# Attention and gated MLP on one Trainium2 core: scores in pairs of tiles, every weight tile turned by DMA, and one division for two heads

## The chip, the cores and the metric

The kernel runs on one core of one Trainium2 chip. The metric is the device time of one execution in microseconds, lower is better. The kernel before takes 2773.86 us (median of three runs, 2771.83 to 2776.18).

## The reference

One transformer block with adaptive layer norm, batch 1, 2048 rows of width 576, all in float32:

```
mod = silu(c) @ w_mod ; sa, ca, ga, sb, cb, gb = six rows of 576
h = layernorm(x) * (1 + ca) + sa
q = h @ wq                                   # 32 heads of 128
k, v = last 512 rows of the caches           # 16 heads, each serves two q heads
p = softmax(q k^T / sqrt(128)) ; o = p v
x = x + ga * (o @ wo)
h = layernorm(x) * (1 + cb) + sb
out = x + gb * ((silu(h @ w1) * (h @ w3)) @ w2)   # hidden width 4608
```

## The kernel before

**Numbers in two halves.** Each float32 operand is split into a high and a low float16 half, and a product is made of three float16 matmuls: high-high, high-low, low-high.

**Attention is cut into 128 slots.** A slot is one query head with one block of 512 rows (`slots`, line 449). Two slots in a row (`j` 0 and 1) are the two heads that share a key head. Each slot has four steps `t`, one for each tile of 128 query rows. The work of several slots is interleaved by the loop at lines 1558 to 1604. Every engine, and SyncE's queue, runs its instructions strictly in the order in which this loop issues them, so the order written there is the schedule. In slot `i` the loop issues:

- `scores(i, t)` in each step (line 475): three matmuls of 512 columns into one bank `pss`; VectorE takes the negated maximum of each row (487) and scales it (488).
- `weights(i, t)` (491): ScalarE takes the exponential out of the bank and sums it (500). For tiles 0 to 2 `half_high` (529) makes the float16 high half on ScalarE and `half_low` (534) the low half on GpSimd; `turn_away` (539) has a DMA transpose, issued by SyncE, turn both halves into the tile `ptw`. Tile 3 is turned by four TensorE transposes (`turn`, 517); ScalarE and VectorE take it out of the bank as high and low halves (525, 549).
- `query(i + 1, part)` (455): 14 matmuls that make the next slot's queries, in three parts (`QP`, 441), then their halves on ScalarE (467) and VectorE (473).
- `values(i - 1)` at the end of the slot (554): 12 matmuls of 512 columns. The first of them already reads all four turned tiles.
- `sums(i - 1, step)` (503): the reciprocal of the row sums, its way through memory (510) and back, spread over all partitions (513).
- `normalize(i - 2)` (567) multiplies the output by that on VectorE; `split_on(i - 2)` (577) in step 3 makes its halves, high on ScalarE (581), low on GpSimd (582).
- `attend_out`, one call in each step (584): six matmuls of 288 columns with `wo`, into the one double bank `E`, and every second step VectorE adds the result to the residual (590).

**The MLP's weights are prepared meanwhile.** Slots 13 to 123 also carry 168 pieces of work that split the weights of the MLP (lines 725 to 736 and 1304 to 1332 give each its due step). A piece of a set of `w1`/`w3` is a ScalarE cast (768) and two GpSimd subtractions (769, 770). `run(i, t)` issues them at the end of a step. After the slots the MLP runs alone.

**Banks.** The eight PSUM banks are `E` (two), `A` (two, for queries and outputs), `S` (two, for scores) and `T` (two, for transposes). `T` also serves the turning of normalized rows (`turn_rows`, 236).

## Time and profile before

| | |
|---|---|
| runs | 2771.83, 2773.86, 2776.18 us |
| the profiled execution | 2773.59 us, span 2771.7 us |
| attention, slots 0 to 127 | 33 to about 1610 us |
| busy TensorE, VectorE, ScalarE, GpSimd | 97%, 72%, 58%, 68% of the span |
| DMA transposes | 384, median 3.9 us from issue to landing |

The profile is one execution, seen by the hardware profiler. Its page gives busy times by engine, the span in 40 slices, and the costliest groups of instructions by line. Other views list groups by form, waits, stretches of time, or instructions in order of time; there a row gives start, duration, engine, line, operation, and out and in operands, and rows of several like instructions are merged (x12). TensorE's matmuls overlap, so the time from start to start is what one costs, not its duration. `PEld` is TensorE's weight load, `POOL` is GpSimd, `ACT` is ScalarE, `DVE` is VectorE and `SPq` is the queue of SyncE.

### The profile page before, as it was taken

What the parts mean: (1) busy time and instruction counts of PE and PEld (TensorE: products, weight loads), DVE (VectorE), ACT (ScalarE), POOL (GpSimd) and SP (SyncE); (2) the same over time, 40 slices, a digit from 0 to 9 for tenths busy, and PEclk for the clock granted to TensorE, in tenths of its full rate; (3) what the DMA queues carried; (4) which work ended last, traced back from release to release, by engine and by line L of the source; (5) the groups of instructions that cost most, each with busy time, mean ns of one, the idle gap of its engine ahead of it and who ended that gap; (6) DMA issues with size and microseconds to landing.
All of it is one profiled execution on the core that took longest, in us unless ns stands there. A gap on an engine that the chain in (4) does not pass through costs nothing.

```text
span 2771.7 us, 44752 instructions
## 1 busy us (share of the span) xinstructions
PE 2692.8 (97%) x15406; PEld 1515.9 (55%) x15406; DVE 1999.8 (72%) x3555; ACT 1617.5 (58%) x3013; POOL 1881.9 (68%) x1748
## 2 busy tenths in 40 slices
PE   6899999999999999999999999999999999999998
PEld 3455555555555555555555555555555555555554
DVE  7877787877788787877876667777776666666666
ACT  5777778777777778787677634544443333333332
POOL 5578788888788877777669537688873465333435
PEclk8999999999999999999999999999999999999999
DMA  5778888788787788979889935656643434333332
GB/s 184 174 174 195 196 177 192 169 184 192 160 185 167 191 186 201 206 182 213 184 190 223 239 112 171 200 170 199 213 135 108 160 121 128 104 103 111 104 110 78
DMA packets 593460, 463.84 MB, mean 167 GB/s; under 512 B 442704, under 2 KB 472528, under 8 KB 592208
## 3 DMA queue, kind: packets, MB, share of 16 engines
q1 hardware_dynamic: 592944, 460.69, 64.9%
q8 instruction: 121, 1.98, 0.3%
q14 instruction: 107, 0.88, 0.1%
q10 hardware_dynamic: 288, 0.30, 0.0%
HBM read 264.19 MB, written 95.99 MB: 130 GB/s over the span
## 4 chain that ended last, share of the span: by engine, by line
PE 52%; DVE 2%; issue 1%; ACT 1%; POOL 1%; DMA 0%; SPq 0%; DVEq 0%; ACTq 0%; POOLq 0%
PE py L847 15%; PE px L847 11%; PE pe L932 7%; PE pf L932 7%; PE pe L433 3%; PE po L562 3%; PE pss L483 3%; PE pq L410 2%; PE pt L523 0%; PE pq L414 0%; DVE table L487 0%; DVE acc L590 0%; DVE on L571 0%; DMA r<-row 0%; ACT p L500 0%
## 5 line engine op out<-in xcount | busy, mean ns | idle before, releaser
L537 POOL TENSOR_TENSOR hp<-p,hp 128x512 f16<-128x512 f32 x384 | 450.2, 1175 | 271.0 <-ACT hp L532 147.9
L500 ACT ACTIVATE p<-pss,table,factors 128x512 f32<-128x512 f32 x512 | 396.9, 775 | 360.9 <-DVE table L488 186.6
L847 PEld LDWEIGHTS <-wset 128*128 128x128 f16 x3528 | 344.6, 98 | 337.9 <-issue 5.3
L487 DVE TENSOR_REDUCE table<-pss 128x1 f32<-128x512 f32 x512 | 350.3, 684 | 209.9 <-PE pss L483 205.9
L847 PE MATMUL py<-hset,wset 128*128 128x512 f16 x2016 | 483.6, 380 | 0.0
L433 PE MATMUL pe<-o 128*128 128x288 f16 x3072 | 459.6, 286 | 15.8 <-DVE acc L590 15.3
L483 PE MATMUL pss<-k,qT 128*128 128x512 f16 x1536 | 420.1, 381 | 13.7 <-ACT p L500 10.3
L433 PEld LDWEIGHTS <-o 128*128 128x128 f16 x3072 | 300.7, 98 | 189.6 <-issue 22.4
L562 PE MATMUL po<-ptw,v 128*128 128x512 f16 x1536 | 359.3, 382 | 10.4 <-DVE ptw L552 5.5
L847 PE MATMUL px<-hset,wset 128*128 128x512 f16 x1512 | 361.6, 379 | 1.6 <-ACT p L500 1.6
L410 PE MATMUL pq<-hT,wq 128*128 128x512 f16 x1092 | 283.2, 382 | 1.0 <-POOL hT L254 0.7
L94 POOL TENSOR_TENSOR akv<-u,akv 128x512 f16<-128x512 f32 x141 | 165.0, 1180 | 174.3 <-ACT akv L93 166.5
L532 ACT CAST hp<-p 128x512 f16<-128x512 f32 x384 | 237.3, 618 | 13.2 <-POOL hT L256 0.6
L562 PEld LDWEIGHTS <-v 128*128 128x128 f16 x1536 | 148.2, 98 | 175.4 <-issue 19.4
L932 PEld LDWEIGHTS <-akv 128*128 128x128 f16 x1728 | 169.6, 98 | 93.8 <-issue 4.8
L483 PEld LDWEIGHTS <-qT 128*128 128x128 f16 x1536 | 147.9, 98 | 129.0 <-issue 15.6
L590 DVE SCALAR_TENSOR_TENSOR acc<-pe,factors,acc 128x576 f32<-128x576 f32 x256 | 207.7, 811 | 10.4 <-PE pe L433 10.4
L582 POOL TENSOR_TENSOR o<-on,o 128x512 f16<-128x512 f32 x128 | 150.4, 1175 | 55.6 <-ACT o L581 52.7
L410 PEld LDWEIGHTS <-wq 128*128 128x128 f16 x1092 | 107.5, 98 | 129.7 <-issue 4.6
L926 DVE SCALAR_TENSOR_TENSOR acc<-pf,table,acc 128x576 f32<-128x576 f32 x140 | 113.4, 810 | 80.3 <-PE pf L932 80.3
L1027 ACT COPY u<-py 128x512 f32<-128x512 f32 x72 | 42.2, 586 | 202.1 <-PE py L847 200.2
L1020 ACT ACTIVATE s<-s,table 128x512 f32<-128x512 f32 x72 | 52.0, 722 | 173.9 <-DVE s L1019 173.9
(244 smaller groups left out, 4791.2 us busy)
## 6 DMA issues: line engine op xcount, KB each, us to landing
wset<-wd SPq DMA_DIRECT2D x213, 320.0 KB, 3.2
r<-row SPq DMA_DIRECT2D x128, 256.0 KB, 3.9
oset<-od SPq DMA_DIRECT2D x106, 288.0 KB, 3.2
wraw<-in_w SPq DMA_DIRECT2D x36, 768.0 KB, 5.7
wd<-wmade SPq DMA_DIRECT2D x75, 320.0 KB, 3.3
wset<-wd SPq DMA_DIRECT2D x71, 160.0 KB, 2.3
w2raw<-in_w SPq DMA_DIRECT2D x19, 576.0 KB, 5.3
wd<-ring SPq DMA_DIRECT2D x33, 320.0 KB, 2.8
```

Of the source, the lines that this page charges most:

```text
L94: eng.tensor_sub(halves[:, 1], src, halves[:, 0])
L410: nc.tensor.matmul(ps, w[:, k // 2, m, :], hT[:, DC + m if k == 1 else m, :], start=s == 0, stop=False)
L433: nc.tensor.matmul(E[:, h, :HALF], o[:, x, rows], w[:, y, h * HALF : (h + 1) * HALF], start=first and n == 0, stop=last and n == 2,)
L483: nc.tensor.matmul(pss, q[:, x, rows], k[:, y, :], start=n == 0, stop=n == 2)
L487: nc.vector.tensor_reduce(nm[:, 0:1], pss, axis=AX.X, op=ALU.max, negate=True)
L500: nc.scalar.activation(p, pss, AF.Exp, bias=nm[:, 1:2], scale=factor, accum_out=st["l"][:, t : t + 1])
L532: nc.scalar.copy(hp[:, 0, :], state[i]["p", t])
L537: nc.gpsimd.tensor_sub(hp[:, 1, :], state[i].pop(("p", t)), hp[:, 0, :])
L562: nc.tensor.matmul(po, v[:, x, c, :], pt[:, y, c, :], start=c == 0 and n == 0, stop=c == KC - 1 and n == 2)
L590: nc.vector.scalar_tensor_tensor(a, E[:, :, :HALF], factors[:, uses[u][0], 2:3], a, op0=ALU.mult, op1=ALU.add)
L847: nc.tensor.matmul(ps, w[:, a, :], h[:, b, :], start=start and n == 0, stop=stop and n == 6, skip_group_check=True)
L932: nc.tensor.matmul(ps[:, h, :HALF], a[:, rows], w[:, b, :], start=m == 0, stop=m == 2)
```

## The change

Four edits belong together:

- **Pairs.** `scores` is issued in steps 0 and 2 only, each time for two tiles, into a pair of banks; one VectorE reduction gives the maxima of both tiles and one instruction scales them. `weights` and `half_high` for both follow in steps 1 and 3. The pairs come from the pool `T`, now two pairs of banks; `S` is gone until the attention has ended.
- **All tiles by DMA.** `turn`, `turn_high` and `turn_low` go. All four tiles pass `half_high`, `half_low` and `turn_away`. The low halves of tiles 0 and 1 are issued at the start of step 2, those of tiles 2 and 3 at the start of the next slot.
- **Low half on VectorE.** The low half of a slot's tile 0 is VectorE's, from slot 3 on.
- **Ratio of sums.** The first head of a pair isn't normalized: ScalarE (`take_first`, step 0) and VectorE make its halves straight from the bank. The second is multiplied by the ratio of the two row sums, and the first head's reciprocal is applied when the result is added to the residual. Reciprocal, row and its return happen once for two slots.

The three parts of the query become 4, 6 and 4 matmul groups instead of 5, 5 and 4.

```diff
-    QP = (range(0, 5), range(5, 10), range(10, 14))
+    QP = (range(0, 4), range(4, 10), range(10, 14))
...
-        pss = bank("S", "pss")
-        for n, (x, y) in enumerate(((0, 0), (0, 1), (1, 0))):
-            nc.tensor.matmul(pss, q[:, x, rows], k[:, y, :], start=n == 0, stop=n == 2)
...
+        pss = pair_bank("pss")
+        for half in range(2):
+            rows = slice((t + half) * P, (t + half + 1) * P)
+            for n, (x, y) in enumerate(((0, 0), (0, 1), (1, 0))):
+                nc.tensor.matmul(pss[:, half, :], q[:, x, rows], k[:, y, :], start=n == 0, stop=n == 2)
...
-        nc.vector.tensor_reduce(nm[:, 0:1], pss, axis=AX.X, op=ALU.max, negate=True)
-        nc.vector.tensor_scalar(nm[:, 1:2], nm[:, 0:1], factor, P_LOG, op0=ALU.mult, op1=ALU.add)
+        nc.vector.tensor_reduce(nm[:, 0:2], pss, axis=AX.X, op=ALU.max, negate=True)
+        nc.vector.tensor_scalar(nm[:, 2:4], nm[:, 0:2], factor, P_LOG, op0=ALU.mult, op1=ALU.add)
...
+        if j == 0:
+            return
         if step == 0:
-            nc.vector.reciprocal(st["l"][:, ST:], st["l"][:, :ST])
+            nc.vector.reciprocal(up, both)
+            nc.vector.scalar_tensor_tensor(ratio, first, O_DOWN, up[:, ST:], op0=ALU.mult, op1=ALU.mult)
...
-        nc.gpsimd.tensor_sub(hp[:, 1, :], state[i].pop(("p", t)), hp[:, 0, :])
+        eng = nc.vector if t == 0 and i > 2 else nc.gpsimd
+        eng.tensor_sub(hp[:, 1, :], state[i].pop(("p", t)), hp[:, 0, :])
...
+    def take_first(i):
+        st = state[i]
+        o = st["o"] = new_o(i)
+        nc.scalar.activation(o[:, 0, :], st["po"], AF.Copy, scale=O_DOWN)
...
     def normalize(i):
         st = state[i]
         po = st.pop("po")
+        if slots[i][1] == 0:
+            o = st["o"]
+            nc.vector.scalar_tensor_tensor(o[:, 1, :], po, O_DOWN, o[:, 0, :], op0=ALU.mult, op1=ALU.subtract)
+            return
...
     for i in range(n + 2):
         run(i, -1)
         for t in range(ST):
+            if t == 0 and 1 <= i <= n:
+                half_low(i - 1, 2)
+                half_low(i - 1, 3)
+            if t == 2 and i < n:
+                half_low(i, 0)
+                half_low(i, 1)
             if t > 1 and i < n:
                 turn_away(i, t - 2)
-            if t == 0 and 1 <= i <= n:
-                turn_away(i - 1, 2)
-            slot, tile = (i - 1 if t == 1 else n, ST - 1)
-            if 0 <= slot < n:
-                turn(slot, tile)
-            if i < n:
+            if t < 2 and 1 <= i <= n:
+                turn_away(i - 1, t + 2)
+            if t % 2 == 0 and i < n:
                 scores(i, t)
...
-            if 1 <= i <= n and t == 2:
-                turn_low(i - 1, ST - 1)
...
-            if i < n:
-                weights(i, t)
-            if t < 3 and i < n:
-                half_high(i, t)
-                half_low(i, t)
-            if t == 1 and 1 <= i <= n:
-                turn_high(i - 1, ST - 1)
+            if t % 2 and i < n:
+                for k in (t - 1, t):
+                    weights(i, k)
+                    half_high(i, k)
+            if 2 <= i <= n + 1 and t == 0 and slots[i - 2][1] == 0:
+                take_first(i - 2)
```

More of the change, by code (lines that the diff above doesn't have):

```diff
@@ L578, in split_on @@
         st = state[i]
+        if slots[i][1] == 0:
+            return
         on = st.pop("on")
-        o = st["o"] = pool.tile([P, 2, SB], F16, tag=("ah", "al")[i % 2], name="o", bufs=3)
+        nc.vector.tensor_scalar(
+            st["l"][:, 5 * ST :], st["l"][:, 2 * ST : 3 * ST], factors[:, uses[slots[i][0]][0], 2:3], 1.0 / O_DOWN,
+            op0=ALU.mult, op1=ALU.mult,
+        )
+        o = st["o"] = new_o(i)
         nc.scalar.copy(o[:, 0, :], on)
@@ L1515, in tile_block @@
         norm_rows(0, t)
-    turned = [turn_rows(0, m, "TTAAS"[m]) for m in range(DC + 1)]
+    firsts = [pair_bank(), pair_bank()]
+    junk = firsts[1][:, 1, :]
+    turned = [
+        turn_rows(0, m, "A", None if m in (2, 3) else firsts[m // 4][:, m % 2, :]) for m in range(DC + 1)
+    ]
     for m in range(DC + 1):
@@ L1607, in tile_block @@
     lane[1] = (E, after.tile([P, 2, 512], F32, tag="T2", name="pf"))
+    later.append(after)
     for _ in stream:
```

53 lines of the change are left out of this document (25 added, 28 removed).

## The prediction

> **What bounds the kernel now.** I read the page first, then busy time by stretches, then one slot in order of time, then groups by line.
>
> ```profile
> span 2771.7 us, 44752 instructions
> ...
> PE 2692.8 (97%) x15406; PEld 1515.9 (55%) x15406; DVE 1999.8 (72%) x3555; ACT 1617.5 (58%) x3013; POOL 1881.9 (68%) x1748
> ...
> PE   6899999999999999999999999999999999999998
> ...
> DMA  5778888788787788979889935656643434333332
> ```
> ```profile
> 242.30:1008.80 766.50, 751.38 (x4289) 418.65 (x4288) 600.71 (x1209) 596.13 (x1154) 651.76 (x627) 1.00 0.80 181
> 1008.80:1293.60 284.80, 280.73 (x1605) 156.16 (x1604) 226.17 (x458) 217.64 (x427) 217.99 (x196) 1.00 0.87 199
> ```
>
> TensorE is busy nearly everywhere. The stretch rows give slots 16 to 79 and 80 to 103: length, then busy TensorE, its weight load, VectorE, ScalarE, GpSimd, clock, DMA share. In the first, TensorE is busy for 98%, VectorE and ScalarE for 78%, GpSimd for 85%, and the DMA engines for 0.80. So TensorE's list of matmuls bounds the attention, at the full clock (1.00), with GpSimd and the DMA engines not far behind. The stretch has 64 slots, so one lasts 766.5 / 64 = 11.98 us. The change leaves the MLP as it is, so only the attention counts.
>
> A slot without delay, in order of time (first column: start):
>
> ```profile
> 611.82 0.81 PE L483 MATMUL pss<-k,qT 128*128 128x512 f16 x3
> ...
> 613.54 0.90 PE L433 MATMUL pe<-o 128*128 128x288 f16 x6
> ...
> 614.28 0.60 PE L523 MATMUL pt<-ident,p 128*128 128x128 f32 x4
> ...
> 614.72 0.81 PE L483 MATMUL pss<-k,qT 128*128 128x512 f16 x3
> ...
> 620.83 2.75 PE L562 MATMUL po<-ptw,v 128*128 128x512 f16 x12
> ...
> 623.42 0.81 PE L483 MATMUL pss<-k,qT 128*128 128x512 f16 x3
> ```
>
> From start to start, twelve matmuls of 512 columns take 2.59 us, 0.216 each; six of 288 take 0.74; the four transposes of tile 3 take 0.44. One slot (611.82 to 623.42) lasts 11.60: 38 x 0.216 + 4 x 0.74 + 0.44 = 11.61. The 0.4 us between that and 11.98 are delays and small other matmuls.
>
> **What the change takes from TensorE.** The four transposes of each of 128 slots: 128 x 0.44 = **56 us**, if nothing else becomes late. A slot would be 11.17. Everything else on TensorE stays.
>
> **The other engines, per slot.**
>
> ```profile
> L537 POOL TENSOR_TENSOR hp<-p,hp 128x512 f16<-128x512 f32 x384 | 450.2, 1175 | 271.0 <-ACT hp L532 147.9 <-issue 81.7 <-DVE table L488 14.2
> ...
> L487 DVE TENSOR_REDUCE table<-pss 128x1 f32<-128x512 f32 x512 | 350.3, 684 | 209.9 <-PE pss L483 205.9 <-PE pe L310 3.2
> ...
> L582 POOL TENSOR_TENSOR o<-on,o 128x512 f16<-128x512 f32 x128 | 150.4, 1175 | 55.6 <-ACT o L581 52.7 <-DMA h<-hf 0.9 <-POOL wmade L770 0.7
> ...
> L571 DVE TENSOR_TENSOR on<-po,r 128x512 f32<-128x512 f32 x128 | 139.0, 1086 | 17.0 <-POOL o L582 8.3 <-DMA r<-row 7.0 <-PE po L562 1.8
> ...
> L488 DVE TENSOR_SCALAR table<-table,factors 128x1 f32<-128x1 f32 x512 | 109.6, 214 | 18.2
> ...
> L769 POOL TENSOR_TENSOR wmade<-wraw,wmade 128x512 f16<-128x512 f32 x99 | 107.1, 1081 | 1.4 <-ACT wmade L768 1.0
> ...
> L552 DVE TENSOR_TENSOR ptw<-pt,ptw 128x512 f16<-128x512 f32 x128 | 87.5, 684 | 27.3 <-ACT ptw L527 25.7 <-DMA od<-omade 1.2
> ...
> L581 ACT CAST o<-on 128x512 f16<-128x512 f32 x128 | 78.1, 610 | 7.1 <-DVE on L571 7.1
> ...
> L768 ACT CAST wmade<-wraw 128x768 f16<-128x768 f32 x99 | 74.4, 751 | 0.0
> ...
> L1126 DVE TENSOR_REDUCE peak_cols<-wraw 128x1 bf16<-128x768 f32 x72 | 67.8, 941 | 0.0
> ...
> L770 POOL TENSOR_TENSOR wmade<-wraw,wmade 64x256 f16<-64x256 f32 x99 | 64.0, 647 | 7.8
> ...
> L1162 DVE TENSOR_REDUCE peak_cols<-w2raw 128x1 bf16<-128x1152 f32 x19 | 25.6, 1346 | 0.1
> ```
>
> - VectorE: a maximum over 1024 columns isn't in the trace; between 941 (768 columns) and 1346 (1152) it is 1.21 us. Two of them for four of 684 save 0.31, two scalings of 214 less save 0.43. Tile 3's low half out of a bank (684) becomes tile 0's out of SBUF: 0.74 to 1.08, by rows further down. A first head's low half is like L552 (684) where 1086 stood: 0.20 a slot. Reciprocal, ratio and factor are a few tiny ones per pair. Net -0.6 us: no new bound.
> - ScalarE swaps one copy for another: nothing.
> - GpSimd keeps three low halves of 1175 a slot and loses L582 for every second slot: -0.59 us.
> - SyncE issues one more transpose, and half the rows of sums and returns. Its other transfers are loads due ten steps later and stores; they can wait.
> - The DMA engines carry a fourth transpose. At 0.80 of 11.98 they work 9.6 us a slot for three transposes and all the rest, so one costs at most 3.2; its 256 KB at the stretch's 181 GB/s are 1.4. Half a return of 256 KB goes. I take +1: (9.6 + 1) / 11.9 = 0.89, and 0.96 from slot 80 on. No bound yet, but landings get later.
>
> **What becomes late: the last tile.** The outputs of slot i (the twelve matmuls) need all four tiles. Tile 3 took a short way over TensorE. Now tiles 2 and 3 go through one long chain. Its pieces, from two other places of the same stretch:
>
> ```profile
> 615.56 0.69 DVE L487 TENSOR_REDUCE table<-pss 128x1 f32<-128x512 f32 x1 [1.49 <-PE pss L483]
> ...
> 616.79 1.16 POOL L537 TENSOR_TENSOR hp<-p,hp 128x512 f16<-128x512 f32 x1
> ...
> 616.99 0.77 ACT L500 ACTIVATE p<-pss,table,factors 128x512 f32<-128x512 f32 x1
> ...
> 617.89 0.62 ACT L532 CAST hp<-p 128x512 f16<-128x512 f32 x1
> ...
> 619.42 0.69 DVE L487 TENSOR_REDUCE table<-pss 128x1 f32<-128x512 f32 x1
> ...
> 620.45 0.78 ACT L500 ACTIVATE p<-pss,table,factors 128x512 f32<-128x512 f32 x1 [0.21 <-POOL hp L537]
> ```
> ```profile
> L544 SPq DMA_TRANSPOSE ptw<-hp x384: 1232/1238/4019, 41.5 to 1592.4; - x192
> ...
> DMA to landing us min/median/max: 3.0/3.9/8.2
> ```
>
> 1. Scores of tiles 2 and 3: six matmuls, 1.29, then 0.2 to the maximum (614.72 + 3 x 0.216 to 615.56). 2. The maximum, 1.21. 3. From its end to the exponential 0.34 (620.11 to 620.45), which holds the scaling. 4. Exponential and high half of a tile, 616.99 to 618.51: 1.52, twice 3.04. Together 6.1. VectorE is late by some 0.5: it must first do tile 0's low half, which stands ahead of this maximum in its queue and itself waits for tile 0's high half and for the residual of step 1. So 6.6.
> 5. GpSimd. Its low halves of tiles 2 and 3 are issued at the start of the next slot, behind all that step 3 gave it. In an even slot that is at best nothing: 1.2 after the last high half. In an odd slot `split_on` stands ahead of them: ScalarE makes that copy after tile 3's high half (0.61), GpSimd then needs 3 x 1.175: **4.2** in all. 6. A transpose takes 1.24 to issue and lands after a median of 3.9 us.
>
> Even slots: 6.6 + 1.2 + 3.9 = 11.7. Odd: 6.6 + 4.2 + 3.9 = 14.7. TensorE meanwhile does, from the start of those scores: 1.29, four query matmuls 0.86, two pieces of `wo` 1.48, values 2.59, then the next slot up to its values: 8.57 (11.17 less 2.59). In all **14.8**. So an even slot has 3 us to spare and an odd one nothing.
>
> A piece of weight preparation in step 3 stands in the same place: 0.75 on ScalarE, then 1.08 + 0.65 on GpSimd. An odd slot becomes 14.7 + 1.73 = 16.4, late by 1.6; an even one 6.6 + 0.75 + 1.73 + 2.35 + 3.9 = 15.3, late by 0.5. By the due times some 48 of the slots 13 to 123 have such a piece in step 3. Sum: 24 odd ones x 1.6 = 38, 24 even x 0.5 = 12, and the 40 other odd ones x 0.4 = 16 (half of the transposes land after the median, up to 8.2). **66 us** of new waits at the values.
>
> **Small terms.**
>
> ```profile
> PE pss L483 <- ACT p L500: 10.3, 15, 2.5
> ...
> PE po L562 <- DVE ptw L552: 5.5, 8, 2.9
> ```
>
> These waits (us, times, longest) go: a pair has two steps until its bank is wanted, and L552 is gone. **-16.** But the turned rows of later blocks, 20 banks of four transposes each, now share the two pairs with the scores. Between nothing and one exponential with its cast (1.5 us) each, I take 0.6: **+12**.
>
> Sum: -56 + 66 - 16 + 12 = +6. Against the profiled execution (2773.59, beside a median of 2773.86): **2780 us**. What TensorE is spared comes back as a wait for the last tile.
>
> **Rivals.**
>
> *The chain fits.* If the chain is 3 us shorter than I think (VectorE not late, GpSimd's list of step 3 mostly done before the last high half, landings at 3.0), the waits vanish: 2773.6 - 56 - 16 + 12 = **2714**; up to 2745 with the waits of the odd slots with a piece partly left. For it: in the trace GpSimd is idle for 271 us ahead of L537, so it has room. This is the side faster than before; it decides if the last transpose lands within 14.8 us of its scores.
>
> *The chain is a microsecond longer.* Then plain odd slots cost 1.2 each (40 x 1.2 = 48), odd ones with a piece 2.6 (62), even ones with a piece 1.5, of which the preceding slot's wait gives back a third (24): 134 - 56 - 16 + 12 = +74, and less some 20 of other delays that are hidden behind these waits: about **2828**. For it: VectorE's new subtraction of two SBUF operands beside GpSimd's:
>
> ```profile
> 611.78 0.92 DVE L386 SCALAR_TENSOR_TENSOR k<-kvraw,us,k 128x512 f16<-128x512 f32 x1
> ...
> 612.24 1.48 POOL L537 TENSOR_TENSOR hp<-p,hp 128x512 f16<-128x512 f32 x1
> ...
> 623.90 0.74 DVE L367 SCALAR_TENSOR_TENSOR v<-kvraw,us,v 128x512 f16<-128x512 f32 x1
> ```
>
> Where both overlapped, GpSimd took 1.48 for 1.16 and VectorE 0.92 for the 0.74 of a like one. The Trainium skill, SBUF — State Buffer, section "SBUF: two separate sides", says that a VectorE operation with two SBUF inputs and a GpSimd operation that reads SBUF exclude each other for a whole instruction; the rows agree in kind. By that rule tile 0's low half can wait for a whole 1.16 and the chain grows by it: this rival's time. DMA shares near 0.96 from slot 80 on speak for it too.
>
> *Nothing to gain.* TensorE's spared time is idle anyway, because jitter of the others sets the slots: within 5 us of **2774**. Against it: many slots run at the 11.6 of the matmuls alone.
>
> **How the numbers follow.** Chances: forecast 0.45 (its own range 2755 to 2808, half a microsecond of chain either way), chain fits 0.30, chain longer 0.15, nothing 0.10. About 0.2%, 5.5 us, is what a measurement can tell. The forecast's range lies for 0.12 below that, 0.12 within, 0.21 above; with the rivals: faster 0.12 + 0.30 + 0.03, same 0.12 + 0.04, slower 0.21 + 0.15 + 0.03. The range from 2714 to 2826 leaves out half of the longest-chain case and a little below the shortest.
>
> **What would show it.** Right: slots of 11.2 us where nothing waits, with no L523; TensorE's longest wait is for `ptw<-hp` ahead of the values, about 50 to 90 us in all, mostly in odd slots and where step 3 has a piece of weights; the pair's maximum takes 1.2. Wrong: that wait is under 20 us and the attention ends near 1555 (the chain fits), or transposes land after 5 us and slots reach 12.5 (the chain is longer), or the wait is elsewhere, ahead of the scores.

## The result and the profile after

| | median us | runs | ratio to before (95% interval) |
|---|---|---|---|
| before | 2772.85 | 2771.61 to 2776.18 (4) | |
| after | 2930.76 | 2927.36 to 2935.35 (4) | 1.0569 (1.0547 to 1.0590) |

The change makes the kernel 5.7% slower, 158 us. The forecast was 2780, with a range up to 2826. The profiled execution of the changed kernel took 2934.12 us.

From the page of the changed kernel:

```profile
span 2932.3 us, 42840 instructions
...
PE 2689.8 (92%) x14894; PEld 1465.9 (50%) x14894; DVE 2066.0 (70%) x3104; ACT 1633.6 (56%) x3013; POOL 1832.6 (62%) x1687
...
PE   6898989879898988989989879999999999999998
...
PE 56%; POOL 12%; DVE 8%; DMA 7%; issue 7%; ACT 3%; SPq 1%; POOLq 0%; ACTq 0%; DVEq 0%
...
L562 PE MATMUL po<-ptw,v 128*128 128x512 f16 x1536 | 406.0, 420 | 176.8 <-DMA ptw<-hp 118.9
L497 DVE TENSOR_REDUCE table<-pss 128x2 f32<-128x1024 f32 x256 | 311.8, 1218 | 333.0 <-PE pss L493 332.3
```

512 instructions left TensorE, as forecast, but its digits in slices 3 to 24, all 9 before, are now 7 to 9, and the chain that ended last, 52% TensorE before with nothing else above 2%, now runs through GpSimd (12%), VectorE (8%) and the DMA engines (7%). Before, the row of the values (L562) read:

```profile
L562 PE MATMUL po<-ptw,v 128*128 128x512 f16 x1536 | 359.3, 382 | 10.4 <-DVE ptw L552 5.5
```

The next fences show the attention and the rest of the span as two stretches, before and after (length, then busy TensorE, weight load, VectorE, ScalarE, GpSimd, granted clock, DMA share, GB/s).

```profile
33.00:1613.20 1580.20, 1533.28 (x8711) 855.97 (x8712) 1211.05 (x2450) 1173.08 (x2271) 1220.96 (x1156) 0.99 0.81 187
1613.20:2771.70 1158.50, 1142.16 (x6618) 647.57 (x6615) 763.26 (x1049) 428.69 (x718) 645.73 (x567) 1.00 0.43 138
```
```profile
33.00:1774.60 1741.60, 1532.71 (x8200) 807.18 (x8200) 1278.50 (x2001) 1189.84 (x2271) 1171.82 (x1096) 0.96 0.79 179
1774.60:2932.30 1157.70, 1140.56 (x6617) 646.92 (x6615) 763.33 (x1050) 428.44 (x718) 645.19 (x567) 1.00 0.44 138
```

The MLP is unchanged. The attention is 161 us longer, although 56 us of transposes are gone, so 217 us came in. Two columns of the L562 rows account for nearly all of it: idle time ahead of the values rose from 10.4 to 176.8, and the values' own matmuls from 359.3 to 406.0, together 213 us. The second part goes with the granted clock, which fell from 0.99 to 0.96. In the trace of the kernel after, the twelve matmuls of the values take 2.37 us from the first start to the last in 85 of the slots 8 to 117, at a granted clock of 1.00, and 3.6 to 4.7 us in the other 25, at 0.50 to 0.66. Of these 25, 24 stand behind more than 2.2 us of idle time, and in the 60 slots with less than 1 us of it the clock is always 1.00. So the lower clock follows the long waits and isn't their cause; it adds 46 us. TensorE's waits in the kernel after (us, times, longest) confirm the place:

```profile
PE po L562 <- DMA ptw<-hp: 118.9, 54, 7.7
PE po L562 <- issue: 30.2, 13, 7.8
PE po L562 <- DMA row<-l: 18.4, 5, 8.6
...
PE pss L493 <- ACT p L511: 6.5, 8, 2.0
```

So the wait that I forecast is there, at the place where I put it, and it is close to three times as long (176.8 for 66). Where the last tile loses its time shows in an even slot, slot 98, on ScalarE, GpSimd and TensorE (three answers of the timeline; start, duration; in square brackets idle time ahead and what ended it):

```profile
1356.46 0.62 ACT L536 CAST hp<-p 128x512 f16<-128x512 f32 x1
1356.98 0.77 ACT L366 ACTIVATE oraw<-oraw,us 128x576 f32<-128x576 f32 x1
1357.79 0.67 ACT L367 CAST o<-oraw 128x576 f16<-128x576 f32 x1
```
```profile
1352.87 1.15 POOL L542 TENSOR_TENSOR hp<-p,hp 128x512 f16<-128x512 f32 x1
1358.54 1.28 POOL L368 TENSOR_TENSOR o<-oraw,o 128x576 f16<-128x576 f32 x1 [4.52 <-ACT o L367]
1359.77 2.28 POOL L542 TENSOR_TENSOR hp<-p,hp 128x512 f16<-128x512 f32 x2
```
```profile
1365.59 2.75 PE L562 MATMUL po<-ptw,v 128*128 128x512 f16 x12 [0.43 <-DMA ptw<-hp]
```

The high half of tile 3 is ready at 1357.08. GpSimd has nothing to do from 1354.02 to 1358.54, but its next instruction is the low half of a piece of the next head's `wo` (L368), which the program issues at the end of the slot, ahead of the low halves of tiles 2 and 3. That piece needs a cast (L367) which stands behind tile 3's high half in ScalarE's queue. The low halves end at 1362.05, 5.0 us after the high half, where I had counted 1.2 for an even slot. The values then wait 0.43 us for the landing, in a slot that I gave 3 us to spare. This piece of `wo` is one kind of work that stands there, in 14 of the 55 even slots from 8 to 117; what stands there in the others is told further down.

### The profile page after: what moved, and what is told of

Its sections match the earlier page's. It is cut to its first block, busy times and chain, and to the rows that moved or that the text cites. A ratio compares the mean times of both kernels' runs of the same rounds, so it can differ in the third digit from the quotient of the medians.

```text
span 2932.3 us, 42840 instructions
## 1 busy us (share of the span) xinstructions
PE 2689.8 (92%) x14894; PEld 1465.9 (50%) x14894; DVE 2066.0 (70%) x3104; ACT 1633.6 (56%) x3013; POOL 1832.6 (62%) x1687
## 4 chain that ended last, share of the span: by engine, by line
PE 56%; POOL 12%; DVE 8%; DMA 7%; issue 7%; ACT 3%; SPq 1%; POOLq 0%; ACTq 0%; DVEq 0%
PE py L865 15%; PE px L865 10%; PE po L562 7%; PE pe L950 6%; PE pf L950 6%; DMA ptw<-hp 5%; POOL hp L542 4%; PE pss L493 4%; PE pe L442 4%; PE pq L419 3%; DVE table L497 2%; ACT p L511 1%; POOL wmade L787 1%; DVE hp L542 1%; DVE table L498 1%
## 5 line engine op out<-in xcount | busy, mean ns | idle before, releaser
L562 PE MATMUL po<-ptw,v 128*128 128x512 f16 x1536 | 406.0, 420 | 176.8 <-DMA ptw<-hp 118.9
L497 DVE TENSOR_REDUCE table<-pss 128x2 f32<-128x1024 f32 x256 | 311.8, 1218 | 333.0 <-PE pss L493 332.3
L542 POOL TENSOR_TENSOR hp<-p,hp 128x512 f16<-128x512 f32 x387 | 456.7, 1194 | 128.1 <-ACT hp L536 101.5
L442 PE MATMUL pe<-o 128*128 128x288 f16 x3072 | 439.7, 286 | 9.6 <-DVE acc L608 8.5
L493 PE MATMUL pss<-k,qT 128*128 128x512 f16 x1536 | 379.4, 383 | 12.3 <-ACT p L511 6.5
L865 PE MATMUL px<-hset,wset 128*128 128x512 f16 x1470 | 351.6, 379 | 0.0
L536 ACT CAST hp<-p 128x512 f16<-128x512 f32 x512 | 316.5, 618 | 60.9 <-DMA ptw<-hp 43.1
L562 PEld LDWEIGHTS <-v 128*128 128x128 f16 x1536 | 155.3, 105 | 388.5 <-issue 194.4
L608 DVE SCALAR_TENSOR_TENSOR acc<-pe,l,acc 128x576 f32<-128x576 f32 x256 | 207.3, 810 | 58.6 <-PE pe L442 39.5
L600 POOL TENSOR_TENSOR o<-on,o 128x512 f16<-128x512 f32 x64 | 74.0, 1156 | 156.4 <-ACT o L599 137.5
```

What stands on the lines that cost most here:

```text
L442: nc.tensor.matmul(E[:, h, :HALF], o[:, x, rows], w[:, y, h * HALF : (h + 1) * HALF], start=first and n == 0, stop=last and n == 2,)
L493: nc.tensor.matmul(pss[:, half, :], q[:, x, rows], k[:, y, :], start=n == 0, stop=n == 2)
L497: nc.vector.tensor_reduce(nm[:, 0:2], pss, axis=AX.X, op=ALU.max, negate=True)
L536: nc.scalar.copy(hp[:, 0, :], state[i]["p", t])
L542: eng.tensor_sub(hp[:, 1, :], state[i].pop(("p", t)), hp[:, 0, :])
L562: nc.tensor.matmul(po, v[:, x, c, :], pt[:, y, c, :], start=c == 0 and n == 0, stop=c == KC - 1 and n == 2)
```

## The experiments

My theory, formed on these traces: the last tile's way through ScalarE, GpSimd, SyncE and the DMA engines is too long for its slot, and most of the excess is the place of the low halves in GpSimd's queue. Rival: a fourth tile by DMA costs about as much wherever its halves stand, because its added work makes other things late. All runs below were timed against the kernel before on the same chip; ratios carry their 95% interval.

| run | median us | ratio to before |
|---|---|---|
| e1 after, low halves of tiles 2, 3 early | 2839.92 | 1.0250 (1.0235 to 1.0265) |
| e2 after, values later | 2958.65 | 1.0676 (1.0660 to 1.0692) |
| e3 e1 and e2 | 2934.62 | 1.0592 (1.0576 to 1.0608) |
| e4 after, all low halves on GpSimd | 2963.50 | 1.0697 (1.0674 to 1.0720) |
| e5 before, tile 3 by DMA, tile 0's low half on VectorE | 2868.86 | 1.0363 (1.0342 to 1.0383) |
| e6 e5 and the ratio of sums | 2835.24 | 1.0228 (1.0211 to 1.0245) |
| e7 before and the ratio of sums | 2767.87 | 0.9986 (0.9977 to 0.9996) |
| e8 e1, values a slot and a half later | 2824.92 | 1.0204 (1.0187 to 1.0220) |
| e9 before, an idle fourth transpose | 2799.96 | 1.0109 (1.0088 to 1.0130) |
| e10 e9 and all idle halves | 2885.43 | 1.0411 (1.0386 to 1.0437) |
| e11 e8, all low halves on GpSimd | 2903.06 | 1.0471 (1.0453 to 1.0490) |
| e12 e9, tile 0's low half on VectorE | 2853.36 | 1.0295 (1.0280 to 1.0311) |
| e13 e9, idle halves of tile 3 | 2852.80 | 1.0293 (1.0277 to 1.0308) |
| e14 e1, VectorE's low half behind the maximum | 2876.08 | 1.0378 (1.0360 to 1.0396) |
| e15 e1, VectorE takes tile 3's low half | 2940.50 | 1.0607 (1.0589 to 1.0624) |
| e16 e1, last two transposes back to back | 2807.54 | 1.0117 (1.0099 to 1.0136) |
| e17 e8, the maximum first on VectorE | 2915.17 | 1.0504 (1.0484 to 1.0524) |
| e18 e16, the same order for tiles 0, 1 | 2823.16 | 1.0189 (1.0175 to 1.0203) |

### Order in the changed kernel: e1 to e4

**e1.** The low halves of tiles 2 and 3 are issued in step 3, right behind their high halves, ahead of `split_on` and the pieces of weights.

```diff
-            if t == 0 and 1 <= i <= n:
-                half_low(i - 1, 2)
-                half_low(i - 1, 3)
...
                     half_high(i, k)
+                if t == 3:
+                    half_low(i, 2)
+                    half_low(i, 3)
```

> The changed kernel with one thing moved: the low halves of tiles 2 and 3 are issued on GpSimd in step 3, right behind their high halves, ahead of split_on and the pieces of weight preparation, instead of at the start of the next slot. In the changed kernel the last low half ends 5.0 us after the last high half (median), and TensorE loses 239 us ahead of the outputs' matmuls. Theory A (GpSimd's order: the last low halves stand behind step 3's list, whose ScalarE parts come after the last high half): the last low half now ends 1.3 us after the high half, the chain from the scores falls from some 17.8 to some 14 us against 14.8 that TensorE has to do, and the time falls by 130 to 180 us, to 2750 to 2800. Rival B (DMA transposes and SyncE's queue are too slow with four a slot): less than 40 us of the 158 come back. Rival C (VectorE's low half of tile 0 makes the second maximum late): less than 40 us come back.

2840 us: 91 of the 158 us go with an order of two instructions on one engine. That is more than the 40 of the rivals and less than the 130 to 180 of theory A: the last low half ends 2.3 us after the last high half in the mean, not 1.3. (The 239 us of this expectation are more than the idle time of 176.8; idle time and the slower matmuls together come near them.) TensorE's wait for the landing falls:

```profile
PE po L562 <- DMA ptw<-hp: 70.4, 37, 5.7
```

**e2, e3.** The values of slot i are issued at the end of step 0 of slot i + 2 (e2), alone and together with e1 (e3).

```diff
             run(i, t)
+            if t == 0 and 2 <= i <= n:
+                values(i - 2)
-        if 1 <= i <= n:
-            values(i - 1)
```

> The changed kernel with the outputs' matmuls of slot i issued at the end of step 0 of slot i + 2 instead of at the end of slot i + 1, and what reads them one step later. TensorE then has 2.9 us more to do before it needs the turned tiles, 17.7 instead of 14.8 us; no engine's work changes. Theory A, or any theory by which the tiles only come late: the waits ahead of the outputs fall from 239 to some 60 us, the time to 2740 to 2790. Rival D (an engine or the DMA engines have no more throughput, or the lower granted clock is the cause and not a consequence): within 40 us of 2931, the wait only moves.

> Both edits together: the last low halves ahead of step 3's list, and the outputs' matmuls a step later. Theory A: a chain of some 14 us against 17.7, so nearly no wait ahead of the outputs, slots of 11.2 us where nothing else waits, and 2715 to 2745, faster than the kernel before (2773) by 1 to 2%. Rival D: over 2850.

Both are slower than the kernel that they start from, and theory A's times are missed by 169 and 190 us; the waits only moved, as rival D said. The waits ahead of the values are gone (0.6 us for a landing in e2), and another has taken their place, as TensorE's waits show, in e2 and then in e3:

```profile
PE pss L493 <- DVE qT L482: 202.9, 116, 5.7
```
```profile
PE pss L493 <- DVE qT L482: 186.9, 115, 5.6
```

The values had stood between the last query matmuls and the next scores, and had covered the time in which ScalarE and VectorE make the query's halves. Moved away, they leave that bare in 116 (e2) and 115 (e3) of 128 slots.

**e4.** Tile 0's low half back on GpSimd.

```diff
-        eng = nc.vector if t == 0 and i > 2 else nc.gpsimd
-        eng.tensor_sub(
+        nc.gpsimd.tensor_sub(
```

> The changed kernel with tile 0's low half back on GpSimd (one part of the change undone). Theory A: the second maximum comes 0.5 to 1 us earlier, but GpSimd has 1.18 us a slot more ahead of the last low halves, so the time stays within 40 us of 2931 or gets longer. Rival C (VectorE's low half is the cause): 2800 or less.

2964 us, 33 above the kernel after. VectorE's low half is not what costs in the changed kernel; GpSimd's time is dearer.

### The parts of the change, put on the kernel before: e5 to e7

**e5.** Tile 3 by DMA and tile 0's low half on VectorE; single tiles, no ratio. GpSimd's low halves stand right behind their high halves. **e6** adds the ratio of sums, so it is the change without pairs. **e7** is the ratio alone.

```diff
-            if t == 0 and 1 <= i <= n:
-                turn_away(i - 1, 2)
-            slot, tile = (i - 1 if t == 1 else n, ST - 1)
-            if 0 <= slot < n:
-                turn(slot, tile)
+            if t < 2 and 1 <= i <= n:
+                turn_away(i - 1, t + 2)
...
-            if t < 3 and i < n:
+            if i < n:
                 half_high(i, t)
-                half_low(i, t)
+                if t:
+                    half_low(i, t)
```

> The kernel before with two of the four edits: tile 3 is turned by DMA as the others, and tile 0's low half is VectorE's, issued at the start of step 2. Scores stay in single tiles, each with its own maximum; every low half on GpSimd is issued right behind its high half. The four TensorE transposes go. Chain of tile 3 by the changed kernel's and the earlier runs' pieces: scores to high half 5.1 us, GpSimd 2.3, SyncE 1.4, landing 4.1, in all 12.9, against 12.3 that TensorE has to do. Theory F (the pairs put both last tiles into one long chain, and that with GpSimd's order makes the loss): waits of 40 to 90 us, time 2750 to 2810. Rival G (a fourth transpose in a slot costs that much whatever the order): over 2850.

> As the run before this one, and the ratio of sums too: three of the four edits, all but the pairs. GpSimd loses 75 us of work, ScalarE's and GpSimd's part of split_on goes in every second slot. Theory F: 10 to 40 us less than without the ratio, 2730 to 2790. Rival G: over 2850.

> The kernel before with the ratio of sums alone. It takes nothing from TensorE, which bounds the attention; GpSimd loses 75 us, VectorE some 10 us, 64 returns of the row sums go. Theory F: within 10 us of the kernel before (2771). Rival H (taking the first head's halves from the bank, with ScalarE ahead of VectorE in step 0, makes later waits): slower by 20 us or more.

e5 fell on the rival's side: without pairs the fourth tile by DMA still costs 98 us in place of bringing 56. e6 fell between the two ranges, e7 inside theory F's. The ratio is the one part that pays: 34 us beside the fourth tile (e6 against e5), 3 to 4 us alone (e7, the only version faster than before, by 0.14%). And e6, without pairs, stands at 1.0228, e1, with pairs and the low halves early, at 1.0250, with overlapping intervals: as far as these two can tell, the pairs themselves cost about nothing. (They differ in more than the pairs: the parts of the query and the place of tile 1's low half.) What cost 91 us was where the low halves stood when the pairs came.

### More distance: e8

The query in two parts of 7 matmul groups in steps 0 and 1, its low half at the start of step 2, the values of slot i at the end of step 1 of slot i + 2, on top of e1.

```diff
-    QP = (range(0, 4), range(4, 10), range(10, 14))
+        return (range(0, 4), range(4, 10), range(10, 14)) if i < 3 else (range(0, 7), range(7, 14))
...
+            if t == 1 and 2 <= i <= n:
+                values(i - 2)
```

> The changed kernel with all four edits and another order: low halves of tiles 2 and 3 right behind their high halves; the query in two parts of 7 matmul groups in steps 0 and 1, its low half at the start of step 2; the outputs' matmuls of slot i at the end of step 1 of slot i + 2, and what reads them in step 2. TensorE then has 19.7 us to do between the scores of tiles 2 and 3 and the outputs, and 6.1 us between the last query matmul and the next scores (5.5 before), so that the wait for the query halves that the later outputs had brought is covered again. Theory A (the tiles only come late for the place at which TensorE wants them): under 20 us of waits ahead of the outputs and under 40 ahead of the scores, 2715 to 2760, faster than the kernel before. Rival D (throughput of an engine, the DMA engines or the clock): over 2850.

2825 us: neither expectation. No landing is late for TensorE now, but its waits, and VectorE's behind them, show that it now waits for VectorE ahead of the pieces of `wo`, and VectorE for ScalarE:

```profile
PE pe L442 <- DVE acc L609: 59.4, 44, 2.8
PE pss L494 <- ACT qT L477: 18.4, 15, 3.6
```
```profile
DVE qT L483 <- ACT qT L477: 89.0, 90, 3.7
...
DVE hp L543 <- ACT hp L537: 56.9, 44, 4.6
```

### Load without a wait: e9, e10, e12, e13

These keep TensorE's turning of tile 3, so its columns of `ptw` are written twice and nothing waits soon for the added transposes or for tile 3's halves. In e10 and e12 tile 0's low half moves to VectorE as well, and that one is read: SyncE's transpose of tile 0 waits for it.

**e9.**

```diff
+        for to in (t, ST - 1) if t == 0 else (t,):
             nc.sync.dma_start_transpose(
-                out=pt.rearrange("p x c n -> p (x c) n")[:, :, t * P : (t + 1) * P],
+                out=pt.rearrange("p x c n -> p (x c) n")[:, :, to * P : (to + 1) * P],
```

> The kernel before, with tile 0's transpose by DMA issued twice in every slot: the second one writes the columns of tile 3, which TensorE's own turning overwrites later, so nothing waits for it soon. It adds a fourth transpose as a load of SyncE's queue and of the DMA engines (128 x 256 KB and 128 issues of 1.24 us) and takes nothing away. Theory W (a fourth transpose costs because TensorE waits for its result, at the end of a long chain in four queues): no landing is late for TensorE, so within 10 us of before, 2763 to 2783. Rival L (the load itself is what costs: the DMA engines and SyncE's queue are so full that all landings get later): over 2800, with transposes that land after a median of 4.5 us or more.

2800 us: 28 us for a result that nobody reads, at the edge of rival L and well above theory W's 2783, though the median landing is 4.1 us and not the 4.5 of the rival. What waits longer is VectorE's normalization for the returned sums (23.8 us, from 7.0) and TensorE for the residual (24.3, from 15.3). Busy time by engine over the same 284.8 us as before shows the DMA share at 0.98, from 0.87:

```profile
1008.80:1293.60 284.80, 278.92 (x1596) 155.13 (x1595) 225.56 (x456) 218.03 (x426) 219.60 (x199) 1.00 0.98 221
```

**e10** adds the idle halves of tile 3 and moves tile 0's low half to VectorE; **e12** has only the second of these, **e13** only the first.

```diff
+            if t == 2 and i < n:
+                half_low(i, 0)
...
-            if t < 3 and i < n:
+            if i < n:
                 half_high(i, t)
-                half_low(i, t)
+                if t:
+                    half_low(i, t)
```

> As the kernel with the idle fourth transpose, and besides with the other work that the change gives to the engines for a tile by DMA: tile 3's high half on ScalarE (0.62 us) and low half on GpSimd (1.17), whose result nobody reads, and tile 0's low half on VectorE in place of GpSimd. TensorE still turns tile 3 itself. So it carries the load of four tiles by DMA, and of the old way of tile 3, without waiting for tile 3's landing. Theory W: 2770 to 2800. Rival L: over 2840 (the kernel before with tile 3 by DMA and TensorE's turning left out measured 2869). Between the two, the part above 2774 is the load's and the rest the wait's.

> The kernel before with the idle fourth transpose (2800 us), and only tile 0's low half moved from GpSimd to VectorE, to the place that the change gives it, ahead of the scores of tile 2. Tile 3 stays wholly with TensorE. Theory V (of the 85 us that the idle halves added, most come from VectorE, which waits in its queue for ScalarE's high half of tile 0 and is late with the next maximum and the residual): 2850 or more. Rival T (they come from tile 3's own halves: 0.62 us more on ScalarE, and GpSimd waiting for the last high half of a slot before it goes on): 2785 to 2815, GpSimd having one low half less.

> The other half of the same split: the kernel before with the idle fourth transpose (2800 us), and tile 3's high half on ScalarE and low half on GpSimd, both read by nobody; tile 0's low half stays on GpSimd, which so makes four of 1.17 us a slot. Theory V: 2800 to 2830 (GpSimd's extra load may cost up to the 33 us that it cost in the kernel after). Rival T: 2860 or more.

e10 takes 2885 us, 113 above before, although nobody reads tile 3's halves: rival L's time holds, and theory W falls. e13, where all the added work is unread, is the cleaner measure of a load: 2853 us, 82 above before. Its load isn't the engines' time alone: ScalarE's high halves wait 45.0 us for one of the four `hp` buffers, which hold a tile's halves until they are turned (34.2 for a landing, 10.8 for GpSimd), where they waited 0.8 for a landing in e9. e5, which reads the fourth transpose and leaves out the old way of tile 3, is 17 us faster than e10. So on the kernel before the added work costs more than e5 loses, and leaving out TensorE's 56 us, with ScalarE's and VectorE's two copies out of the bank, pays back only 17. The 85 us that e10 has above e9 don't belong to one of the two parts: each alone gives 53 (2853 and 2853). Theory V held in e12 and failed in e13; Rival T failed in e12 and missed e13 by 7 us. How the queues carry such work on shows in the waits of e12, SyncE's first. VectorE's low half holds SyncE's queue, which needs both halves of tile 0 before it can issue anything behind them: 317.7 us, and 39.2 for GpSimd's low halves, where e9 has 184.3 for GpSimd's alone. TensorE then meets late low halves of tile 3, which it turned itself (34.6 us, from 7.6 in e9), and late landings (18.1, from 7.3), neither of which the edit touched; its wait for the residual is that of e9 (24.3):

```profile
SPq L546 <- DVE hp L538: 317.7, 111, 7.2
```
```profile
PE po L564 <- DVE ptw L554: 34.6, 37, 3.5
PE pe L433 <- DVE acc L592: 25.2, 23, 6.5
PE po L564 <- DMA ptw<-hp: 18.1, 10, 6.8
```

### Other places for the low halves: e11, e14, e15, e17

**e11** is e8 with tile 0's low half on GpSimd (the diff of e4).

> The kernel of two slots' distance (query in two parts, values a slot and a half later, GpSimd's halves ahead of its other work; 2825 us), with tile 0's low half back on GpSimd. If VectorE is late with the residual there because tile 0's low half and its wait for ScalarE (57 us) stand in VectorE's queue, as I think, then the waits ahead of the pieces of wo (about 90 us above the kernel before) lose half or all: 2735 to 2790. Rival: GpSimd's fourth low half of 1.17 us delays its other work as much (in the kernel after it cost 33 us): 2815 or more, with the waits ahead of pe for VectorE as they were.

2903 us: the rival. VectorE has less to do, and still the query's low half waits for ScalarE, whose own waits show why it is late: its high halves need one of the four `hp` buffers, and these come free later, since GpSimd and so the transposes are later (110.3 us, from 33.7 in e8; the query's low half waits 294.2 for ScalarE, from 89.0):

```profile
ACT hp L537 <- DMA ptw<-hp: 110.3, 79, 4.3
```

**e14** is e1 with tile 0's low half, and the transposes of tiles 0 and 1, behind the maximum of tiles 2 and 3.

```diff
             if t % 2 == 0 and i < n:
                 scores(i, t)
+            if t == 2 and i < n:
+                half_low(i, 0)
+                half_low(i, 1)
+            if t > 1 and i < n:
+                turn_away(i, t - 2)
```

> The kernel after with GpSimd's halves of tiles 2 and 3 issued early (2840 us), and VectorE's low half of tile 0 issued behind the maximum of tiles 2 and 3 in place of ahead of it, the transposes of tiles 0 and 1 with it. In that kernel the maximum ends 4.0 us after its scores start, against 2.7 at the least. If VectorE's low half makes it late, the chain of the last tile gets about 1.2 us shorter and the waits ahead of the values (142 us) lose half: 2770 to 2805. Rival: the maximum is late for other work of VectorE, and then nothing changes: 2825 to 2855.

2876 us, a miss for both. The maximum did come earlier (3.3 us after its scores start in place of 4.0, means over slots 8 to 117), but the transposes of a slot go out in order, and the last one now left 2.2 us after its low half in place of 1.4: SyncE's queue was held longer by tile 0, as its waits show (210.5 us in e1).

```profile
SPq L549 <- DVE hp L542: 340.0, 103, 9.1
```

**e15** is e1 with VectorE making tile 3's low half and GpSimd the others.

```diff
-        eng = nc.vector if t == 0 and i > 2 else nc.gpsimd
+        eng = nc.vector if t == ST - 1 and i > 2 else nc.gpsimd
```

> The same kernel (2840 us), with VectorE making the low half of tile 3, behind the residual of step 3, and GpSimd those of tiles 0, 1 and 2. The last two low halves of a slot then run side by side on two engines, and no low half stands ahead of a maximum within its slot: last high half to last low half 1.2 us in place of 2.3, and the maximum of tiles 2 and 3 a microsecond earlier. If the chain of the last tile is what costs: 2730 to 2790. Rival: VectorE, held by its wait for the last high half, is late with the first maximum and the query halves of the next slot, and the waits move ahead of the scores: 2840 or more.

2941 us. The last low half came 1.0 us after its high half, as meant, and the transpose 3.6 us after that: it stood behind those of tiles 0 to 2, for which GpSimd was now late (SyncE's queue waits 584.7 us for GpSimd's low halves, 284.1 in e1). The time is the rival's, but the mechanism isn't: the waits stayed ahead of the values (85.6 us for landings) and came ahead of the residual's bank (55.8). **e17** puts the maximum first in VectorE's queue of e8's step 2, and the other operations behind it.

```diff
+            if t % 2 == 0 and i < n:
+                scores(i, t)
             if t == len(parts_of(i + 1)) and i + 1 < n:
                 query_low(i + 1)
```

> The kernel of two slots' distance (2825 us), with the maximum of tiles 2 and 3 first in VectorE's queue of step 2, and the query's low half, the normalization and tile 0's low half behind it; the transposes of tiles 0 and 1 move behind them too. There the values come late enough that a late transpose costs nothing (1.7 us of waits ahead of them). If what holds that kernel is VectorE's order (ScalarE waits 282 us for the scaled maximum, and TensorE 111 for the residual and VectorE's other work): 2750 to 2800. Rival: every reordering moves the lateness on to the next operation in the same queue, here the query's halves and the residual: 2815 to 2850.

2915 us: past the rival. Each operation moved behind is late in turn (`PE pss L494 <- DVE qT L483: 74.1, 110, 2.7`, and SyncE's queue waits 451.7 us for VectorE's low half, 110.9 in e8).

### SyncE's queue: e16, e18

**e16** is e1 with both last transposes at the start of the next slot.

```diff
-            if t < 2 and 1 <= i <= n:
-                turn_away(i - 1, t + 2)
+            if t == 0 and 1 <= i <= n:
+                turn_away(i - 1, 2)
+                turn_away(i - 1, 3)
```

> The kernel after with GpSimd's halves of tiles 2 and 3 issued early (2840 us), and the transposes of tiles 2 and 3 issued one behind the other at the start of the next slot, so that SyncE's loads and stores of step 0 no longer stand between them. There the last transpose is issued 1.4 us after its low half is ready, which I had counted at nothing. If SyncE's queue is a term of the chain: that time falls to 0.5 us or less, the waits ahead of the values (142 us) to some 90, and the time to 2780 to 2815. Rival: SyncE only waits for GpSimd, and the transposes of a slot are held up by each other (each takes 1.24 us to issue): 2830 to 2850.

2808 us, inside the theory's range: 32 us for the loads and stores of one step that stood between two transposes. The time from the last low half to its transpose fell from 1.4 to 1.0 us in the mean and from 1.1 to 0.6 in the median. That is less than the fall to 0.5 us that I expected, and it is only part of what the chain gained: the landing got shorter too (table below).

**e18** does the same for tiles 0 and 1: GpSimd's low half of tile 1 in step 1, both transposes at the start of step 2.

```diff
             if t == 2 and i < n:
                 half_low(i, 0)
-                half_low(i, 1)
-            if t > 1 and i < n:
-                turn_away(i, t - 2)
+                turn_away(i, 0)
+                turn_away(i, 1)
```

> The kernel with the transposes of tiles 2 and 3 back to back (2808 us), and the same two steps for the first two tiles: GpSimd's low half of tile 1 right behind its high half in step 1, ahead of the pieces of weights, and the transposes of tiles 0 and 1 back to back at the start of step 2, ahead of SyncE's loads and stores. In that kernel GpSimd starts tile 1's low half 2.7 us after it could, and the transpose of tile 2 waits 0.5 us behind that of tile 1. If the order of GpSimd's and SyncE's queues is what costs: 2760 to 2795. Rival: what is left of the waits ahead of the values (98 us) comes from the maximum and the high halves, which this doesn't touch, or goes to the pieces that now come later: 2795 to 2825.

2823 us, the rival. TensorE's waits, of e16 first and then of e18, show that less is waited for landings again, but more for VectorE's residual:

```profile
PE po L562 <- DMA ptw<-hp: 67.3, 31, 6.2
PE pe L442 <- DVE acc L608: 12.3, 14, 2.0
```
```profile
PE po L562 <- DMA ptw<-hp: 52.7, 31, 6.2
PE pe L442 <- DVE acc L608: 33.3, 33, 3.2
```

## Why the prediction was wrong, step by step

The chain of the last tile, from the start of the scores of tiles 2 and 3 to the landing of tile 3, read from the start and end times of the trace, mean over slots 8 to 117, in us. In brackets stands the forecast's mean over all even and all odd slots, with the pieces of weights that it counted:

| | forecast | after | e4 | e15 | e14 | e1 | e18 | e16 |
|---|---|---|---|---|---|---|---|---|
| scores to last high half | 6.6 | 7.9 | 7.7 | 8.4 | 7.6 | 7.9 | 8.4 | 8.0 |
| to last low half | 1.2 even, 4.2 odd (with pieces 2.6, 4.8) | 5.0 | 5.3 | 1.0 | 2.4 | 2.3 | 2.1 | 2.3 |
| to its transpose | 0 | 1.05 | 1.2 | 3.6 | 2.2 | 1.4 | 0.7 | 1.0 |
| to its landing | 3.9 | 3.8 | 4.0 | 4.2 | 4.1 | 4.1 | 4.0 | 3.8 |
| sum | 11.7, 14.7 (with pieces 13.1, 15.3) | 17.8 | 18.1 | 17.1 | 16.3 | 15.7 | 15.3 | 15.2 |
| time | 2780 | 2931 | 2964 | 2941 | 2876 | 2840 | 2823 | 2808 |

- **What TensorE is spared**: right. 512 instructions fewer, and slots in which nothing waits last 11.14 to 11.2 us (11.17 forecast).
- **The failed step is GpSimd's term of the even slots**: "In an even slot that is at best nothing: 1.2". Over all even slots, with the pieces that I counted, that makes 2.6 in the mean; it measured 4.6. So the even slots wait nearly as much as the odd ones: the idle time ahead of the values is 80.3 us in even and 96.4 in odd slots, where I had put 12 and 54. The pieces that I counted are there as forecast: of the 55 even slots from 8 to 117, 21 have a piece with a ScalarE cast in step 3 (24 of 64 forecast). What I left out is the rest of what the program gives GpSimd there. Sums and gates that GpSimd makes alone for the MLP's weights (L780 to L782, L831 to L839; they aren't among the 168 pieces) end behind the last high half in 14 even slots, the low half of a piece of `wo` (L368) in 14, a piece from step 2 in 5. So the best case, nothing else behind the last high half, holds in 13 slots (1.4 us in the mean); with work of the MLP's weights alone it is 5.2 us (28 slots), with L368 alone 5.0 (6), with both 7.6 (8). L368 also shows that an idle GpSimd can have to wait: it is tied to a ScalarE instruction behind the last high half. In odd slots the forecast was nearer: 5.3 in the mean for 4.8, and 4.0 in most of the 25 slots with `split_on` alone (4.2 forecast; its sum, 0.61 + 3 x 1.175, is 4.1).
- **SyncE at nothing**: wrong by 1.05 us. "Its other transfers ... can wait" is true of them, but they don't wait: they stand ahead of the last transpose. e16 shows that step alone at 32 us.
- **Scores to high half**: 7.9 for 6.6. The maximum ended 4.0 us after the scores began, where 3.2 was forecast, and ScalarE's four steps took 4.0 for 3.4. Half of that is a wait that I didn't look for: four `hp` buffers serve four tiles a slot now, three before, and ScalarE's high halves wait 43.1 us for a landing to free one, 34.6 of them on tiles 2 and 3 (before there is no such wait). A kernel with more buffers was not tried.
- **Landing**: right (3.8 for 3.9). The slots reached 12.6 us in the median without the late landings that I had named as the sign of a longer chain.
- **The sum of the small terms** (-16 and +12) hardly mattered: the scores' wait for the exponential went from 10.3 to 6.5, and the turned rows showed no new wait of size.
- **The price of a microsecond**: near. My rival "the chain is a microsecond longer" put it at 48 us (2828 against 2780). A straight line through the seven kernels of the table rises by 51 us per us of mean chain. The chain was 5.8 us longer than forecast in plain even slots and 3.4 in plain odd ones, not one, and so the time left the range. But the same line gives 2798 at 14.8 us (an estimate, just outside the chains measured), where my sum without waits gives 2714. So the zero of the sum is off as well: a chain that fits wouldn't by itself have made the kernel faster, as far as these seven tell.
- **Means against spread**: the plan of 14.8 us for the chain is met in the mean by e16 to 0.4 us, and it still waits 67 us for landings. In its trace the landing of tile 3 lies between 17.4 and 24.2 us after the slot's start (5th and 95th percentile). My sum compared two fixed numbers and added 0.4 us for the spread.
- **GpSimd and VectorE excluding each other**: VectorE's low half did take longer, 1.02 us in the mean of 125 (0.67 to 2.34), where in e14, at another place, it takes 0.74. The rule of the Trainium skill, SBUF — State Buffer, section "SBUF: two separate sides", agrees in kind with that row. What it costs was not measured by itself: e4, which takes VectorE's subtraction away and gives GpSimd a fourth one, is 33 us slower: on VectorE, with the exclusion, the low half is still the cheaper of the two.
- **The DMA engines and the load**: the shares forecast for four transposes, 0.89 and 0.96, were near (e9, with all returns kept: 0.91 from 242 to 1008 us, 0.98 from slot 80 on). In the kernel after the share over the attention is only 0.79, because the slots got longer: 0.79 x 1741.6 us against 0.81 x 1580.2 before is 0.75 us a slot more, for +1 forecast. "No bound yet" was too kind: e9 lost 28 us by a fourth transpose alone. My sum had no term for added work that nobody waits for; e9 and e13 show 28 and 82 us of it on the kernel before.
- **The rivals**: "the chain fits" would have needed 14.8; no version in the table reached it in the mean. That nothing was to be gained because other engines set the slots was rejected from the trace of before, where waits were small; e12 and e13 show how thin that was: a low half more on VectorE, or a high and a low half more on ScalarE and GpSimd, about a microsecond a slot on each, cost 53 us above e9.

**What is shown and what isn't.** Shown: the added time lies at the values; 91 us of it is GpSimd's order (e1), 32 more SyncE's (e16); with both mended the change still costs 34 us, and on the kernel before the added work costs 82 with nothing of it read (e13), 113 with tile 0's low half on VectorE besides (e10). These don't add up to one account, since each mended wait uncovers the next. Open: which engine sets the remaining 34 us of e16, and whether an order exists in which the spared 56 us come out; none of those tried here is one. Pairs with tile 3 left on TensorE were not tried, nor more `hp` buffers.

## What to carry to other kernels

When a result is moved from the bottleneck engine to a chain over several in-order queues, list for each queue everything that the program issues between the chain's link and the instruction ahead of it, and what each of these waits for; an idle engine is no proof that it will take the link at once. Test the load by itself first: issue the new work with its result unread, and see whether the time holds. And put the chain's links first in every queue they pass, before looking for more distance: here two moved lines on GpSimd and SyncE were worth 123 us, and moving the reader later cost 28 us (e2), because it had been covering another latency.

## What the runs showed of the hardware that was not expected

- The granted clock sinks behind long waits of TensorE and not behind short ones: in the kernel after, twelve matmuls take 2.37 us in all 60 slots with less than 1 us of idle time ahead of them, and 4.1 us in the mean of the 22 with more than 2.5 us, at a mean clock of 0.61. Over the attention the clock is 0.99 before and 0.96 after.
- A transpose whose columns are overwritten later costs 28 us per 128 of them on this kernel, with the DMA share at 0.98 in the densest stretch and a median landing of 4.1 us against 3.9. Whether SyncE's queue, which issues it for 1.24 us, or the DMA engines make the cost was not separated.
